# Loading and transforming the first batch of a spectral layer in finer pieces, with its weights behind the input and its tables placed by halves

## The chip, the cores and the metric

The kernel runs on one core of a Trainium2 chip. The metric is the device time of one execution in microseconds (us). TensorE is also called PE here (PEld is its weight load), VectorE is DVE, ScalarE is ACT, GpSimd is POOL and SyncE is SP, as the profile names them.

## The reference

```python
# x (8, 3008, 256); w_r, w_i (256, 256); b_r, b_i (256)
X = np.fft.rfft(x, axis=1);  Xr, Xi = X.real, X.imag
Yr = Xr @ w_r - Xi @ w_i + b_r
Yi = Xr @ w_i + Xi @ w_r + b_i
Y  = soft-threshold of Yr and Yi at 0.01
y  = np.fft.irfft(Y, n=3008, axis=1)
# then, over all 24064 rows of y, w_in (256, 2048), w_out (2048, 256)
r = np.maximum(y @ w_in, 0.0)
out = (s * r * r + b) @ w_out
```

## The kernel before

The length of 3008 is split as 94 x 32. The first DFT, over n1 (94 values), is a matmul with the table A_t. Its result ut is multiplied by W ("mix", into g), in pieces that are counted by u. A second DFT, over n2 (32 values), uses the tables F_t and F_2 and yields z after the soft threshold. The inverse DFT uses T_t. Then the MLP follows, which is most of the time. The first batch runs alone, in an order of its own; the batches behind it are woven into the MLP.

The tables are loaded in a compact form (F_c, T_c) and *placed* on the chip into zeroed tiles (F_t, F_2, T_t). W is loaded as f32 (w_st) and placed as f16 (W_t). The 256 features stand in two halves of 128, counted by dc. To evacuate a matmul's result is to copy it out of the accumulator (psh and the like), on ScalarE or VectorE.

```python
def emit_load_x(b):                       # GpSimd's queue, f32 -> f16
    for c in range(N2 // XCH):            # 4 chunks of XCH = 8 n2
        t = xpool.tile([P, XCH * D], F16, name="x16", tag="x16")
        nc.gpsimd.dma_start(out=t[0:N1, :], in_=xv[:, c * XCH * D : (c + 1) * XCH * D])
...
emit_load_x(0)
for w in (w_r, w_i):                      # SyncE's queue, beside x
    st = rpool.tile([P, DC, D], F32, name="w_st", tag="rt")
    nc.sync.dma_start(out=st, in_=w.rearrange("(c p) e -> p c e", p=P))
...
def first_batch():
    keep_awake(44)                        # matmuls on ones, for the clock
    for c in range(N2 // XCH):
        for dc in range(DC):
            ...                           # 8 matmuls into two banks
            for h in range(2):
                ... evac(ut[:, dc, :, n2 : n2 + 4], ...)   # ScalarE or VectorE
        keep_awake(18 if c < 3 else 12)
        if c == 1: ... emit_load_forward()                 # F_c, after this chunk's VectorE copies
        if c == 2: ... emit_load_inverse()                 # T_c
        if c == 2: ... place_w()                           # ScalarE
    place_f()                             # ScalarE, F_t from F_c
    place_f_2(0)                          # VectorE
    ...
    for i in range(2 * U + 2):            # U = 6; g of every third u is copied by ScalarE
        mix(*steps[i]); fwd_dft(*steps[i - 1]); inv_dft(*steps[i - 2]); ...
        if i == 0: ... place_t(0)         # VectorE
        if i == 2: ... place_f_2(1); place_t(1)
```

Of the kernel before, what the change touches and what calls it, by code (L numbers as in the profile page):

```python
# [14 lines left out]
P = 128  # L15
N1 = 94
N2 = 32
# [79 lines left out]
def kernel(  # L97
# [13 lines left out]
    nc = tc.nc  # L111
    B, S, D = x.shape
# [5 lines left out]
    H = NPAIR // 2  # L118
# [36 lines left out]
    def evac(dst, src, cols, scale=None):  # L155
        ta, td = 0.17 + cols / 1200.0, 0.15 + cols / 960.0
        if load["act"] + ta <= load["dve"] + td:
            load["act"] += ta
            if scale is None:
                return None, nc.scalar.copy(out=dst, in_=src)  # L160
            return None, nc.scalar.mul(out=dst, in_=src, mul=scale)
        load["dve"] += td
        if scale is None:
            return nc.vector.tensor_copy(out=dst, in_=src), None
        return nc.vector.tensor_scalar_mul(out=dst, in0=src, scalar1=scale), None

    def two_banks():
        return hpool.tile([P, 2, 512], F32, name="psh", tag="psh")
# [8 lines left out]
    XCH = 8  # L177
    x16 = {}

    def emit_load_x(b):  # L180
        xv = x[b].rearrange("(n1 n2) d -> n1 (n2 d)", n2=N2)
        for c in range(N2 // XCH):
            t = xpool.tile([P, XCH * D], F16, name="x16", tag="x16")
            nc.gpsimd.dma_start(  # L184
                out=t[0:N1, :], in_=xv[:, c * XCH * D : (c + 1) * XCH * D]
            )
            x16[(b, c)] = t

    ones = cpool.tile([P, P], F16, name="ones")
# [2 lines left out]
    def keep_awake(n):  # L192

        ps = other_bank()
        for _ in range(n):
            nc.tensor.matmul(ps[:, 0:P], ones, ones, start=True, stop=True)
# [6 lines left out]
    w_st = []  # L203
    for w in (w_r, w_i):
        st = rpool.tile([P, DC, D], F32, name="w_st", tag="rt")
        nc.sync.dma_start(out=st, in_=w.rearrange("(c p) e -> p c e", p=P))
        w_st.append(st)

    b_g = cpool.tile([P, 2, D], F32, name="b_g")
    nc.vector.memset(b_g, 0.0)  # L210
# [52 lines left out]
    nc.vector.memset(T_t, 0.0)  # L263
    F_2 = [uspool.tile([P, H, P], F16, name="F_2", tag="us") for _ in range(2)]
    for f in F_2:
        nc.vector.memset(f, 0.0)

    def make_bounds():
        for t, c in ((low, -LAM), (high, LAM)):
# [11 lines left out]
    def blocks(t):  # L281
        return t.rearrange("p q (r a k) -> p q r a k", r=2, a=2)

    def place_w():
        for i in range(2):
            nc.scalar.copy(out=W_t[:, :, i], in_=w_st[i])

    def place_f():
        for a in range(2):
            r = slice(64 * a, 64 * a + 64)  # L290
            nc.scalar.copy(out=blocks(F_t)[r, :, :, a], in_=F_c[r])

    def place_f_2(h):

# [8 lines left out]
    def place_t(h):  # L303
        q = slice(h * H, h * H + H)
        for i in range(4):
            r = slice(32 * i, 32 * i + 32)
            c = 64 * (i % 2)
            nc.vector.tensor_copy(out=T_t[r, q, c : c + 64], in_=T_c[r, q])
# [20 lines left out]
    def first_batch():  # L329
        ut = ypool.tile([P, DC, 96, N2], F16, name="ut", tag="yt")  # L330
        last_dve = last_act = None
        keep_awake(44)
        for c in range(N2 // XCH):
            for dc in range(DC):
                ps = two_banks()
                for j in range(XCH):
                    lo = j * D + dc * P
                    last_pe = nc.tensor.matmul(
                        ps[:, j // 4, (j % 4) * 96 : (j % 4) * 96 + 96],
                        x16[(0, c)][0:N1, lo : lo + P], A_t[0:N1, :],  # L340
                        start=True, stop=True,
                    )
                for h in range(2):
                    n2 = c * XCH + 4 * h
                    on_dve, on_act = evac(
                        ut[:, dc, :, n2 : n2 + 4],
                        ps[:, h, 0:384].rearrange("p (n k) -> p k n", k=96), 384,
                    )
                    last_dve = on_dve or last_dve
                    last_act = on_act or last_act  # L350
            with tc.issue_after(last_pe.ins):
                keep_awake(18 if c < 3 else 12)
            if c == 1:
                with tc.issue_after(last_dve.ins):
                    nc.vector.memset(F_c[0:1, 0, 0, 0:1], 0.0)
                emit_load_forward()
            if c == 2:
                with tc.issue_after(last_dve.ins):
                    nc.vector.memset(T_c[0:1, 0, 0:1], 0.0)
                emit_load_inverse()  # L360
            if c == 2:
                with tc.issue_after(last_act.ins):
                    place_w()
        with tc.issue_after(last_dve.ins), tc.issue_after(last_act.ins):
            place_f()
            place_f_2(0)

        gate = nc.gpsimd.tensor_copy(out=w_in_t[0][0:1, 0:1], in_=T_c[0:1, 0, 0:1])
# [11 lines left out]
        def mix(ec, u):  # L380
            ps = two_banks().rearrange("p h (j r e) -> p (h j) r e", j=2, r=2)
            for j in range(4):
                q = 4 * u + j
                for dc in range(DC):
                    nc.tensor.matmul(  # L385
                        ps[:, j], ut[:, dc, 4 * q : 4 * q + 4, :],
                        W_t[:, dc, :, ec * P : (ec + 1) * P],
                        start=(dc == 0), stop=(dc == DC - 1),
                    )
            g = vpool.tile([P, 4, 2, P], F16, name="g0", tag="v")  # L390
            if u % 3 == 1:
                nc.scalar.copy(out=g, in_=ps)
                load["act"] += 1.02
            else:
                g_last[0] = nc.vector.tensor_tensor(  # L395
                    out=g, in0=ps,
                    in1=b_g[:, :, ec * P : (ec + 1) * P].unsqueeze(1).to_broadcast([P, 4, 2, P]),
                    op=ALU.add,
                )
                load["dve"] += 1.2  # L400
            gs[(ec, u)] = g
# [83 lines left out]
        for i in range(2 * U + 2):  # L485
            if i < 2 * U:
                mix(*steps[i])
            if 0 <= i - 1 < 2 * U:
                fwd_dft(*steps[i - 1])
            if 0 <= i - 2 < 2 * U:  # L490
                inv_dft(*steps[i - 2])
            k = i - U - 2
            if 0 <= k < 4:
                turn(0, k)
            if 0 <= k - 1 < 4:
                last_dft(0, 8 * (k - 1))
            if i >= 2 * U:
                some(3)
            if i == 0:
                with tc.issue_after(g_last[0].ins):  # L500
                    place_t(0)
            if i == 2:
                with tc.issue_after(g_last[0].ins):
                    place_f_2(1)
                    place_t(1)
            if i == 9:

                gate = nc.gpsimd.tensor_copy(out=low[0:1, 0, 0:1], in_=vt[0:1, 1, 0, 0:1])
                with tc.issue_after(gate.ins):
                    make_w_g()  # L510
                    make_bounds()
# [377 lines left out]
```

## Time and profile before

| | before |
|---|---|
| time | 854.56 us, median of 3 executions (854.24 to 855.53); 854.43 with three more, run beside the changed kernel |
| span in the profile, TensorE busy | 853.9 us, 98% |
| first MLP matmul (L730) | 52.31 us in this profile |
| from there to the end of the span | 801.6 us |

A line of the timeline reads: start, length, engine, source line, operation, what it writes and reads, shapes, count, and in brackets how long the engine was idle before it and what ended that. "Stretches" are slices of 2 us with the busy time of PE, PEld, DVE, ACT and POOL (and their instruction counts), then the granted clock, the DMA share and GB/s.

The profiled execution itself took 855.68 us.

### The profile page before, as it was taken

How to read it: one execution, taken by the hardware profiler on the slowest of the kernel's cores; microseconds unless marked ns; L12 is line 12 of the kernel's file. 1: busy time of each engine (PE TensorE's matmuls, PEld its weight loads, DVE VectorE, ACT ScalarE, POOL GpSimd, SP SyncE). 2: the span in 40 equal slices, each digit the busy share in tenths (PEclk: the TensorE clock that was granted, in tenths of full speed). 3: DMA queues.
4: the chain of work that ended last, by engine and by line, in shares of the span. 5: the costliest groups of instructions: out<-in, count | busy, mean ns of one | idle time of the engine just before them, and what ended most of it. 6: DMA issues, size and time to landing. Idle time of an engine off the chain costs nothing.

```text
span 853.9 us, 17140 instructions
## 1 busy us (share of the span) xinstructions
PE 838.1 (98%) x6690; PEld 603.6 (71%) x6690; DVE 698.1 (82%) x1025; ACT 643.0 (75%) x856; POOL 32.4 (4%) x54
## 2 busy tenths in 40 slices
PE   8889999999999999999999999999999999999997
PEld 7757777777777766777667776777667777766765
DVE  6888987888878887888878888888977888776674
ACT  5688887787778887787777887787877778666663
POOL 3210000000000000000000000000000000000000
PEclk9999999999999999999999999999999999999999
DMA  7863456423672357423662247613354223411111
GB/s 170 154 148 100 102 157 172 121 75 94 169 191 62 93 138 198 113 80 97 164 174 78 75 106 183 186 41 90 101 154 118 63 78 96 112 32 38 38 44 50
DMA packets 104866, 95.07 MB, mean 111 GB/s; under 512 B 9422, under 2 KB 97234, under 8 KB 103442
## 3 DMA queue, kind: packets, MB, share of 16 engines
q1 hardware_dynamic: 98786, 79.57, 32.2%
q0 software_dynamic: 6000, 14.42, 10.6%
q8 instruction: 52, 0.85, 0.4%
q14 instruction: 28, 0.23, 0.1%
HBM read 52.54 MB, written 46.66 MB: 116 GB/s over the span
## 4 chain that ended last, share of the span: by engine, by line
PE 90%; DVE 4%; ACT 3%; DMA 1%; issue 1%; POOL 0%; DVEq 0%; ACTq 0%; POOLq 0%
PE psa L799 37%; PE psh L730 37%; PE psf L596 4%; PE psf L531 3%; PE psf L567 2%; PE psf L582 2%; PE psf L626 2%; PE psf L679 2%; DVE gt L744 1%; DMA x<-in_x_dram 1%; ACT rt L737 1%; PE psh L385 1%; DVE g L395 1%; ACT yt L160 1%; PE psf L416 0%
## 5 line engine op out<-in xcount | busy, mean ns | idle before, releaser
L737 ACT ACTIVATE rt<-psh 128x1024 f32<-128x1024 f32 (+2 forms) x384 | 387.1, 1009 | 115.7 <-PE psh L730 114.5
L744 DVE TENSOR_TENSOR gt<-rt 128x1024 f16<-128x1024 f32 (+2 forms) x323 | 386.6, 1200 | 99.3 <-ACT rt L737 98.7
L799 PE MATMUL psa<-w_out_t,gt 128*128 128x256 f16 (+1 forms) x3024 | 453.9, 272 | 0.1
L799 PEld LDWEIGHTS <-gt 128*128 128x128 f16 (+1 forms) x3024 | 301.0, 101 | 186.9 <-issue 1.7
L730 PE MATMUL psh<-yt,w_in 128*128 128x512 f16 (+1 forms) x1344 | 396.9, 378 | 0.0
L730 PEld LDWEIGHTS <-w_in 128*128 128x128 f16 x1536 | 142.7, 98 | 26.6 <-issue 1.7
L809 DVE SCALAR_TENSOR_TENSOR ost<-psa,s_bc,bias_bc 128x512 f32<-128x512 f32 (+1 forms) x96 | 70.9, 738 | 9.6 <-PE psa L799 8.2
L741 ACT ACTIVATE gt<-rt 128x1024 f16<-128x1024 f32 (+2 forms) x61 | 64.1, 1051 | 1.0
L601 DVE TENSOR_TENSOR ring<-psf,s 128x512 f16<-128x512 f32 x84 | 57.5, 685 | 3.5 <-PE psf L596 3.4
L160 ACT CAST v<-psf 128x512 f16<-128x512 f32 x80 | 46.5, 582 | 18.1 <-PE psf L626 18.1
L160 ACT CAST xf<-psf 128x512 f16<-128x512 f32 x82 | 48.0, 585 | 11.1 <-PE psf L567 11.1
L160 ACT CAST u<-psf 96x512 f16<-96x512 f32 x78 | 45.1, 580 | 12.3 <-PE psf L531 12.1
L730 PE MATMUL psh<-tail,w_in 128*128 128x512 f16 (+1 forms) x192 | 52.1, 353 | 0.0
L596 PE MATMUL psf<-W_g,xf 128*128 128x256 f16 x336 | 50.4, 273 | 0.0
L160 ACT CAST yt<-psf 128x480 f16<-128x480 f32 (+2 forms) x76 | 38.5, 518 | 14.4 <-PE psf L679 14.3
L531 PE MATMUL psf<-x,A_t 94*96 94x512 f16 x104 | 39.6, 381 | 1.7 <-ACT yt L160 0.5
L607 DVE TENSOR_TENSOR ring<-ring,high 128x512 f16<-128x512 f16 x84 | 35.5, 423 | 2.2
L608 DVE TENSOR_TENSOR ring<-ring 128x512 f16<-128x512 f16 x84 | 35.5, 422 | 1.9
L606 DVE TENSOR_TENSOR ring<-ring,low 128x512 f16<-128x512 f16 x84 | 35.4, 422 | 1.5
L596 PEld LDWEIGHTS <-xf 128*128 128x128 f16 x336 | 32.9, 98 | 3.7
L184 POOL DMA_DIRECT2D x<-in_x_dram x32 | 16.8, 526 | 461.3 <-PE psf L531 445.1
L679 PE MATMUL psf<-C_t,vs 96*128 96x96 f16 x448 | 32.9, 205 | 0.0
(83 smaller groups left out, 492.2 us busy)
## 6 DMA issues: line engine op xcount, KB each, us to landing
out_dram<-ost SPq DMA_DIRECT2D x152, 128.0 KB
x<-in_x_dram POOLq DMA_DIRECT2D x32, 376.0 KB, 5.8
ud<-u SPq DMA_DIRECT2D x28, 384.0 KB
us<-ud SPq DMA_DIRECT2D x28, 384.0 KB
vd<-v SPq DMA_DIRECT2D x42, 256.0 KB
vs<-vd SPq DMA_DIRECT2D x14, 768.0 KB
ring<-ring SPq DMA_DIRECT2D x280, 32.0 KB
out_dram<-ost SPq DMA_DIRECT2D x16, 120.0 KB
```

Source lines behind the costliest of these rows:

```text
L160: return None, nc.scalar.copy(out=dst, in_=src)
L531: nc.tensor.matmul(ps[0:96, :], A_t[0:N1, :], x16[(b, c)][0:N1, j * D : (j + 2) * D], start=True, stop=True,)
L596: nc.tensor.matmul(ps[:, r, :], xt[:, 2 - r, dc], W_g[:, dc, r], start=(dc == 0), stop=(dc == DC - 1),)
L601: nc.vector.tensor_tensor(out=t, in0=ps, in1=hold[i // 2][:, i % 2].unsqueeze(1).to_broadcast([P, 2, D]), op=ALU.add,)
L607: nc.vector.tensor_tensor(out=m, in0=m, in1=high, op=ALU.min)
L679: nc.tensor.matmul(ps[:, j * 96 : (j + 1) * 96], vs[(b, h)][:, k, ec * P : (ec + 1) * P], C_t, start=True, stop=True,)
L730: nc.tensor.matmul(o, w_in_t[dc][:, mc * P : (mc + 1) * P], r, start=(dc == 0), stop=(dc == DC - 1),)
L737: nc.scalar.activation(out=rt[:, :, 0:w], in_=ps[:, :, 0:w], func=AF.Relu)
L741: nc.scalar.activation(out=gt[:, :, 0:w], in_=rt[:, :, 0:w], func=AF.Square)
L744: nc.vector.tensor_tensor(out=gt[:, :, 0:w], in0=rt[:, :, 0:w], in1=rt[:, :, 0:w], op=ALU.mult)
L799: nc.tensor.matmul(ps[0:size, h, :], gts[(ti, mc // 2)][:, mc % 2, sub * size : (sub + 1) * size], w_out_t[:, mc, :], start=(mc == 0), sto ...
L809: nc.vector.scalar_tensor_tensor(out=ost[0:size, 0:k], in0=ps[0:size, 0:k], scalar=s_bc[0:size], in1=bias_bc[0:size, 0:k], op0=ALU.mult, o ...
```

## The change

Its intent is to start TensorE on x earlier and to keep the first batch from waiting for tables. x of batch 0 is loaded in halves of a chunk; the first DFT goes in groups of 4 n2, of which dc 0 is evacuated by ScalarE and dc 1 by VectorE; W is loaded behind the second group instead of beside x, and in halves; F_t and T_t are placed by halves; and the F_2 memsets go to GpSimd. The lines that only rename or regroup are cut.

```diff
     def emit_load_x(b):
+            parts = 2 if b == 0 else 1
+            w = XCH * D // parts
+            for i in range(parts):
+                nc.gpsimd.dma_start(... halves ...)
 ...
-        nc.sync.dma_start(out=st, in_=w.rearrange("(c p) e -> p c e", p=P))
+    def emit_load_w():
+        for e in (slice(0, P), slice(P, D)):
+            for w, st in zip((w_r, w_i), w_st):
+                nc.sync.dma_start(
+                    out=st[:, :, e], in_=w.rearrange("(c p) e -> p c e", p=P)[:, :, e]
+                )
 ...
-        nc.vector.memset(f, 0.0)          # F_2
+        nc.gpsimd.memset(f, 0.0)
 ...
-        keep_awake(44)
-        for c in range(N2 // XCH):
+        keep_awake(30)
+        for g in range(N2 // 4):
+            c, h = divmod(g, 2)
 ...                                       # 4 matmuls and one copy per dc
-                keep_awake(18 if c < 3 else 12)
+                keep_awake(7)
+            if h == 0:
+                continue
+            if c == 0:
+                with tc.issue_after(last_dve.ins):
+                    for st in w_st:
+                        nc.vector.memset(st[0:1, :, 0:D:P], 0.0)
+                emit_load_w()
 ...
             if c == 2:
                 with tc.issue_after(last_act.ins):
-                    place_w()
+                    place_w(0)
         with tc.issue_after(last_dve.ins), tc.issue_after(last_act.ins):
-            place_f()
+            place_w(1)
+            place_f(0)
 ...
+            if i == 1: ... place_f(1)
             if i == 2:
                     place_f_2(1)
+            if i == 3:
                     place_t(1)
```

More of the change, by code (lines that the diff above doesn't have):

```diff
@@ L183, in emit_load_x @@
             t = xpool.tile([P, XCH * D], F16, name="x16", tag="x16")
-            nc.gpsimd.dma_start(
-                out=t[0:N1, :], in_=xv[:, c * XCH * D : (c + 1) * XCH * D]
-            )
+            parts = 2 if b == 0 else 1
+            w = XCH * D // parts
+            for i in range(parts):
+                nc.gpsimd.dma_start(
+                    out=t[0:N1, i * w : (i + 1) * w],
+                    in_=xv[:, c * XCH * D + i * w : c * XCH * D + (i + 1) * w],
+                )
             x16[(b, c)] = t
@@ L205 @@
         st = rpool.tile([P, DC, D], F32, name="w_st", tag="rt")
-        nc.sync.dma_start(out=st, in_=w.rearrange("(c p) e -> p c e", p=P))
         w_st.append(st)
+    def emit_load_w():
[3 more added lines that the diff above has]
+                    out=st[:, :, e], in_=w.rearrange("(c p) e -> p c e", p=P)[:, :, e]
+                )
     b_g = cpool.tile([P, 2, D], F32, name="b_g")
@@ L282, in blocks, with place_w, place_f @@
         return t.rearrange("p q (r a k) -> p q r a k", r=2, a=2)
-    def place_w():
+    def place_w(ec):
+        e = slice(ec * P, ec * P + P)
         for i in range(2):
-            nc.scalar.copy(out=W_t[:, :, i], in_=w_st[i])
-    def place_f():
+            nc.scalar.copy(out=W_t[:, :, i, e], in_=w_st[i][:, :, e])
+    def place_f(h):
+        q = slice(h * H, h * H + H)
         for a in range(2):
             r = slice(64 * a, 64 * a + 64)
-            nc.scalar.copy(out=blocks(F_t)[r, :, :, a], in_=F_c[r])
+            nc.scalar.copy(out=blocks(F_t)[r, q, :, a], in_=F_c[r, q])
     def place_f_2(h):
@@ L331, in first_batch @@
         last_dve = last_act = None
-        keep_awake(44)
-        for c in range(N2 // XCH):
+        keep_awake(30)
+        for g in range(N2 // 4):
+            c, h = divmod(g, 2)
             for dc in range(DC):
-                ps = two_banks()
-                for j in range(XCH):
-                    lo = j * D + dc * P
+                ps = two_banks()[:, 0]
+                for j in range(4):
+                    lo = (4 * h + j) * D + dc * P
                     last_pe = nc.tensor.matmul(
-                        ps[:, j // 4, (j % 4) * 96 : (j % 4) * 96 + 96],
+                        ps[:, j * 96 : j * 96 + 96],
                         x16[(0, c)][0:N1, lo : lo + P], A_t[0:N1, :],
@@ L342, in first_batch @@
                     )
-                for h in range(2):
-                    n2 = c * XCH + 4 * h
-                    on_dve, on_act = evac(
-                        ut[:, dc, :, n2 : n2 + 4],
-                        ps[:, h, 0:384].rearrange("p (n k) -> p k n", k=96), 384,
-                    )
-                    last_dve = on_dve or last_dve
-                    last_act = on_act or last_act
-            with tc.issue_after(last_pe.ins):
-                keep_awake(18 if c < 3 else 12)
+                on_dve, on_act = evac(
+                    ut[:, dc, :, 4 * g : 4 * g + 4],
+                    ps[:, 0:384].rearrange("p (n k) -> p k n", k=96), 384,
+                )
+                last_dve = on_dve or last_dve
+                last_act = on_act or last_act
+            with tc.issue_after(last_pe.ins):
+                keep_awake(7)
[6 more added lines that the diff above has]
+                emit_load_w()
             if c == 1:
@@ L391, in mix @@
             if u % 3 == 1:
-                nc.scalar.copy(out=g, in_=ps)
+                g_last[0] = nc.scalar.copy(out=g, in_=ps)
                 load["act"] += 1.02
@@ L501, in first_batch @@
                     place_t(0)
+            if i == 1:
+                with tc.issue_after(g_last[0].ins):
+                    place_f(1)
             if i == 2:
@@ L504, in first_batch @@
                     place_f_2(1)
+            if i == 3:
+                with tc.issue_after(g_last[0].ins):
                     place_t(1)
```

## The prediction

> **What bounds the kernel now.** I read the page first, then the chain of waits that ended last over the first 60 us, then the timeline of the first 40 us, then the clock by stretches of 2 us. The page's first lines say where time can be won:
>
> ```profile
> span 853.9 us, 17140 instructions
> ...
> PE 838.1 (98%) x6690; PEld 603.6 (71%) x6690; DVE 698.1 (82%) x1025; ACT 643.0 (75%) x856; POOL 32.4 (4%) x54
> ...
> PE 90%; DVE 4%; ACT 3%; DMA 1%; issue 1%; POOL 0%; DVEq 0%; ACTq 0%; POOLq 0%
> ```
>
> TensorE is busy 98% of the span and is 90% of the last chain. The change touches only the first batch, up to about 54 us, where the long run of L730 and L799 begins. After that the order of instructions of the two kernels agrees on every engine (line numbers aside). So the change can only shift when the long TensorE phase starts, by less than the some 20 us in which the first batch waits for something. 2% would be 17.1 us; that is out of reach.
>
> In the first 26 us the last chain reads (start, length, what):
>
> ```profile
> 1.87 7.16 DMA x<-in_x_dram
> ...
> 11.15 0.04 DVE F_c L355
> 11.21 3.68 DMA F_c<-dft_fwd
> ...
> 14.96 1.47 ACT F_t L291
> 16.45 1.47 ACT F_t L291
> ...
> 24.38 1.24 DVE g L395
> ```
>
> So it is: the load of x; the VectorE copies of ut (10.13 to 11.15) that let a memset release the load of F_c; that load; the placing of F_t on ScalarE in two pieces of 1.47 us; the mix copy g behind it (17.94), for which the forward DFT waits until 17.97; then VectorE, where four T_t pieces (22.90 to 24.35) stand ahead of the next g. The timeline adds how the four chunks of x arrive and what TensorE does:
>
> ```profile
> 6.59 0.85 PE L338 MATMUL psh<-A_t,x 94*128 94x96 f16 x16 [0.67 <-DMA x<-in_x_dram]
> ...
> 13.08 0.85 PE L338 MATMUL psh<-A_t,x 94*128 94x96 f16 x16
> ...
> 14.14 1.02 DVE L164 CAST ut<-psh 128x384 f16<-128x384 f32 x2 [0.97 <-ACT ut L160]
> ...
> 24.55 0.49 PE L385 MATMUL psh<-W_t,ut 128*128 128x256 f16 x3 [1.10 <-ACT g L392]
> ```
>
> Chunks start on TensorE at 6.59, 9.07, 11.09 and 13.08, two us apart, although nothing on TensorE holds them: x comes at the pace of the DMA engines. The last ut copy ends at 14.14 + 1.02 = 15.16, 2.1 us after its chunk began, because VectorE waits for ScalarE (the releaser in brackets). The clock by stretches (PEclk is the value after the POOL counts) has one hole:
>
> ```profile
> 26.00:28.00 2.00, 2.00 (x19) 1.42 (x17) 1.18 (x3) 1.16 (x2) 0.00 (x0) 0.65 1.05 207
> 28.00:30.00 2.00, 2.00 (x17) 1.69 (x16) 1.38 (x2) 1.16 (x2) 0.00 (x0) 0.50 1.09 219
> ```
>
> The granted clock halves from about 26.7 to 30.1 us, after the idle TensorE of 24 to 26 us (0.83 of 2 us busy).
>
> **What the Trainium skill says.** "TensorE: Matmul & The Clock Gate", part 1, "The HAM clock gate": the clock is half until a busy window of 3413 ns has passed, and falls back after an idle one; the window runs free of the kernel. The trace agrees: the 44 first matmuls on ones take 4.61 us, 105 ns each, the later ones 57 ns each (18 in 1.03 us), and the hole is 3.4 us long. The keep-awake matmuls serve this, and the change cuts them. "DMA: Bandwidth & Descriptors", "Queues, rings and completion order": each DMA engine goes round robin between the rings it has work for. The records agree in part: from 6 to 8 us W and x packets alternate (14 of 1024 B to 12 of 4096 B in a quarter us), but from 4.0 to 5.0 us x went almost alone. "VectorE: DVE Perf Modes", "Zero memsets can be issued as uint32": a memset takes one cycle per element, so as uint32 it has half the elements. VectorE's memset of one F_2 half is 128x768 uint32 at 0.75 us. On GpSimd it is 128x1536 f16; I estimate 1.3 to 1.8 us each, no run so far shows it.
>
> **The change part by part.**
>
> 1. x in halves. A chunk is 94 packets of 4096 B at 0.322 us over 16 engines, 1.9 us; a half is 94 packets that I estimate at 0.165 us, 0.97 us. The first group can start after one half, and W (512 KB, 512 packets of 1024 B at 46 ns, 1.5 us of all engines) no longer goes ahead. With a first packet at 2.9 us and 0.65 us from the last packet to TensorE (as at 12.4 to 13.08 now), groups land at 4.5, 5.5, 6.5 us and so on. TensorE starts 2.1 us earlier than 6.59.
>
> 2. W moves behind the second group: issued at about 7.5, first packet 1.1 us later as F_c shows (11.21 to 12.3), at 8.6. It is now 1024 packets of 512 B. The us loads at 65 to 70 us are such packets: 27 ns each. That is 1024 x 27 / 16 = 1.7 us, 0.2 more than before. Interleaved with the rest of x it delays the end of x by about 0.5 us: 2.9 + 7.8 + 0.5 = 11.2, last group on TensorE at 11.9 against 13.08. The first halves of W land at about 12.4, all of W at 13.3.
>
> 3. The copies side by side. dc 0 goes to ScalarE, dc 1 to VectorE, each waiting for TensorE alone; after the last matmul 1.2 us instead of 2.1. Taken alone this gives ut at 13.1. But ScalarE is strict in order, and its W placing (two copies, about 0.4 us each) stands ahead of the last two groups' copies. It can't start before 12.4. So ScalarE copies group 6 at 13.2, group 7 at 13.9, and mix starts at about 14.7 against 14.76 and 15.21 now. **Most of the 2 us of the x load is lost here**: 0.3 us is left.
>
> 4. F_c queues behind W in the same ring. All bytes before it are those of before, plus 0.2 us for smaller packets; it lands at about 15.1, not 14.88. Cost 0.2 us.
>
> 5. Tables by halves. F_t(0) is two pieces of 0.74 us, 1.47 us less ahead of g on ScalarE, less 0.3 for W's second half: F_t(0) ends at 16.7 instead of 17.92. The first mix copy on VectorE ends at 15.2 + 0.9 + 1.24 = 17.3, so the forward DFT begins at 17.4 instead of 17.97. Gain 0.55 us.
>
> 6. T_t(1) moves behind u = 3. VectorE now runs T_t(0) to 18.8, g to 20.0, two z to 21.3, F_2(1) to 22.15, g(3) to 23.4. Before, g(3) ended at 25.62. Gain 2.2 us on that g; the T_t(1) pieces come after z(2), 24.1 to 25.5, and hold z(3) to 25.6 against 27.02: of the 2.2 about 1.4 to 1.6 us stays.
>
> 7. Clock. TensorE is no longer idle around 24 to 26 us, so the hole should not follow. In it the chain was on TensorE from 25.66; up to 1.7 us (half of 3.4) could be won, much of it hidden behind ScalarE and VectorE; I count 0.5 us.
>
> 8. GpSimd memsets: 5 to 10 us, ahead of F_2 at 15.2: hidden. Two VectorE memsets of 0.75 us leave before the first group, where they would delay the copy of 5 us.
>
> Sum: the gains of 1 to 5 are the 0.55 us at the forward DFT; with part 6, 1.5 us; with the clock 2.0. I take off 0.4 us for my own optimism (no waits between parts): **1.6 us, 854.56 - 1.6 = 853.0 us**.
>
> **Rivals.**
> A. The W placing is the new wait. If W lands at 13 or later, ScalarE keeps groups 6 and 7, TensorE idles from 11.6 to 13.7, and a clock window falls in it: then the mix matmuls run at half clock, 16 x 0.11 us becomes 3.5 us, and 1.5 us goes. For it: the fewer keep-awake matmuls (86 against 110), and that W is strictly behind x. Against it: a window with 72% busy (9.66 less 6.25, 2.46 us of 3.41) kept the clock. It makes 854.5 to 855.
> B. W lands by 12, because it takes its turns between the x packets fully, as in 6 to 8 us now. Then nothing of part 3 is lost, ut is there at 13.2, and F_c becomes the only bound: 851 to 852.
> C. The first 50 us are hidden anyway, by the load of x(1) and the MLP weights that starts when T_c lands. Against it: those are issued by 22 us and land by about 39, and their first reader stands at 45 us. The chain from 34 to 54 us runs over TensorE, ScalarE and VectorE in turn, with no DMA in it. I give it little.
>
> **Range and chances.** Run to run 854.24 to 855.53, the clock window being free-running. My parts are uncertain by 0.5 us at the landing of W and of F_c and by 1 us at the clock. 851.2 to 854.9 should hold 8 in 10. Either 2% bound would need 17 us: 0.5% each.
>
> **What would show it.** x: first L338-type matmul at 4.5 us instead of 6.59, groups about 1 us apart. W: the ScalarE copy W_t waits for DMA at 10.5 to 12.5, and the copies of ut behind it start late. F_c landing at 15.0 to 15.3. Forward DFT at 17.4, the fourth g ended at 23.4, first L730 at about 50.5 instead of 52.31. Clock: no half-clock stretch between 20 and 35 us. It is wrong if a half-clock stretch falls on the mix (rival A), if ut is complete before 13.5 (rival B), or if first L730 moves and the end does not (rival C).

## The result, and the profile after

The changed kernel took 854.8 us (median of 6 fast executions, 854.4 to 857.06), the kernel before 854.43 (854.16 to 855.53) in the same rounds. The ratio is 1.0006, 95% interval 0.9993 to 1.0019: the same. Ratios here are the mean time of one kernel's fast runs over the mean of the other's fast runs of the same rounds, so not quite the ratio of the medians. The forecast was a gain of 1.6 us; none came.

The page of the changed kernel, with the lines that answer to those of before:

```profile
span 853.2 us, 17109 instructions
...
PE 836.9 (98%) x6666; PEld 601.8 (71%) x6666; DVE 696.9 (82%) x1025; ACT 644.0 (75%) x860; POOL 37.3 (4%) x60
...
PE 91%; DVE 4%; ACT 3%; DMA 1%; issue 1%; DVEq 0%; ACTq 0%; POOLq 0%
```

Nothing on the page tells the kernels apart. The chain of waits over the first 30 us does (start, length, what):

```profile
7.63 5.77 DMA w_st<-in_w_r_dram
...
13.49 0.16 ACT W_t L299
...
14.63 0.78 PE psh L353 x8
...
16.16 2.77 PE psh L406 x16
...
18.95 1.01 ACT g L413
```

Before, this stretch of the chain ran over x, the ut copies and F_c. Now it runs over **the load of W**, issued at 7.63 and landed 5.77 us later, then over ScalarE's placing of W, a copy of ut, the last x group (at 14.63) and the mix. The timeline shows how one waits for the other:

```profile
4.85 0.51 PE L353 MATMUL psh<-A_t,x 94*128 94x96 f16 x8 [0.43 <-DMA x<-in_x_dram]
...
13.49 0.71 ACT L299 CAST W_t<-w_st 128x256 f16<-128x256 f32 x2 [1.97 <-DMA w_st<-in_w_r_dram]
...
14.11 0.47 ACT L160 CAST ut<-psh 128x384 f16<-128x384 f32 x1
14.63 0.78 PE L353 MATMUL psh<-A_t,x 94*128 94x96 f16 x8 [2.00 <-ACT ut L160]
...
15.95 2.96 PE L406 MATMUL psh<-W_t,ut 128*128 128x256 f16 x16
...
19.18 0.22 PE L437 MATMUL psf<-g,F_t 128*128 128x128 f16 x1 [0.26 <-DVE g L416]
```

ScalarE stands 1.97 us before W_t although its next copy of ut, behind it in its order, could run. TensorE then stands 2.00 us for that copy. The first group did start early (4.85, before 6.59), but the last one started at 14.63, later than before (13.08). The 16 mix matmuls took 2.96 us. In the stretches, the clock tells why (first the kernel before, then the changed one):

```profile
14.00:16.00 2.00, 1.67 (x20) 1.23 (x18) 1.78 (x6) 1.52 (x3) 0.00 (x0) 1.00 0.77 216
16.00:18.00 2.00, 1.06 (x11) 0.71 (x9) 1.79 (x3) 1.97 (x3) 0.60 (x2) 1.00 0.49 134
```

```profile
14.00:16.00 2.00, 1.37 (x16) 1.36 (x15) 0.55 (x1) 1.45 (x5) 0.00 (x0) 0.67 0.82 288
16.00:18.00 2.00, 2.00 (x12) 1.41 (x10) 0.96 (x6) 1.87 (x3) 0.40 (x2) 0.50 0.36 110
```

The granted clock is 0.67 and 0.50 where before had 1.00 from 14 to 18 us. In this execution no hole follows at 26 to 30 us; half clock lies on the mix instead. The load of F_c, which queues behind W, came late too. VectorE, which reads F_c beside ScalarE, waited for it until 16.29 us, where in the kernel before F_c had landed at 14.89 (11.21 + 3.68):

```profile
16.29 0.25 DVE L312 TENSOR_SCALAR F<-F_c 64x384 f16<-64x384 f16 x1 [0.29 <-DMA F_c<-dft_fwd]
```

The profile of before was of one of the longer executions, so I ran that kernel once more, unchanged, to have one of a common execution (854.30 us, a single run, so its state is unknown):

> The kernel before, unchanged, for a second trace. Of its ten timed executions two took 855.3 to 855.7 us, and eight 854.1 to 854.5; the first profile came from one of the two slow ones and has a half-clock stretch from 26.7 to 30.1 us. If the stretch is what made it slow, this profile, if it falls among the common ones, shows no half clock between 6 and 850 us, the same times up to 25 us (forward DFT at 17.9 to 18.1) and the first matmul of the MLP at 50.8 to 51.2 us instead of 52.3, with the span at 852.4. If the common executions differ earlier than 25 us, the stretch was not the cause.

Its stretch after 26 us, and its first MLP matmul beside that of the first profile and that of the changed kernel:

```profile
26.00:28.00 2.00, 1.98 (x27) 1.54 (x25) 1.18 (x3) 1.26 (x3) 0.00 (x0) 1.00 1.08 215
...
51.03 0.38 PE L730 MATMUL psh<-yt,w_in 128*128 128x512 f16 x1
```

```profile
52.31 0.38 PE L730 MATMUL psh<-yt,w_in 128*128 128x512 f16 x1
```

```profile
51.71 0.38 PE L756 MATMUL psh<-yt,w_in 128*128 128x512 f16 x1
```

In the common execution of before the clock is 1.00 there, although TensorE had been even less busy just before, from 24 to 26 us (0.72 of 2 us, against 0.83 in the first profile). In the changed kernel it is idle there as well (0.92 of 2 us busy). First the common execution of before, then the changed kernel:

```profile
24.00:26.00 2.00, 0.72 (x8) 0.52 (x8) 1.96 (x4) 0.60 (x1) 0.00 (x0) 1.00 1.03 205
```

```profile
24.00:26.00 2.00, 0.92 (x13) 0.70 (x11) 1.96 (x5) 1.74 (x3) 0.00 (x0) 1.00 1.08 215
```

The MLP of the common execution starts 1.3 us earlier than in the profile that the prediction was read from. Against the common one, the changed kernel starts its MLP 0.68 us *later* (51.71 against 51.03). From the first MLP matmul to the end of the span it is 801.5 us in both.

### The profile page after: what moved, and what is told of

It is laid out like the page before. It is cut to its first block, busy times and chain, and to the rows that moved or that the text cites. A ratio compares the mean times of both kernels' runs of the same rounds, so it can differ in the third digit from the quotient of the medians.

```text
span 853.2 us, 17109 instructions
## 1 busy us (share of the span) xinstructions
PE 836.9 (98%) x6666; PEld 601.8 (71%) x6666; DVE 696.9 (82%) x1025; ACT 644.0 (75%) x860; POOL 37.3 (4%) x60
## 4 chain that ended last, share of the span: by engine, by line
PE 91%; DVE 4%; ACT 3%; DMA 1%; issue 1%; DVEq 0%; ACTq 0%; POOLq 0%
PE psa L825 37%; PE psh L756 37%; PE psf L622 4%; PE psf L557 3%; PE psf L593 2%; PE psf L608 2%; PE psf L652 2%; PE psf L705 2%; DVE gt L770 1%; ACT rt L763 1%; PE psh L406 1%; DMA w_st<-in_w_r_dram 1%; ACT yt L160 1%; ACT vs L160 0%; DMA x<-in_x_dram 0%
## 5 line engine op out<-in xcount | busy, mean ns | idle before, releaser
L160 ACT CAST u<-psf 96x512 f16<-96x512 f32 x78 | 45.1, 580 | 12.3 <-PE psf L557 12.1
L187 POOL DMA_DIRECT2D x<-in_x_dram x36 | 18.9, 528 | 461.2 <-PE psf L557 445.1
```

Of the source, the lines that this page charges most:

```text
L160: return None, nc.scalar.copy(out=dst, in_=src)
```

## The experiments

All kernels gave correct results. Kernels named together ran on the same chip and share the runs of the kernel before (854.2 to 854.3 us in each series). There are four series: e1 to e4; e5 to e8; e9, t1 and x1 with the repeat above; t2 and t3. The first three ran on one chip, the fourth on another. Of the ten runs of before that e5 to e8 are compared with, nine are those of e1 to e4. "Slower" and "faster" below mean an interval that leaves out 1.

### First series: the wait for W, and the clock

**e1, W placed after all x groups** (changed kernel with one edit). It takes away ScalarE's wait in the middle of the x groups.

```diff
-            if c == 2:
-                with tc.issue_after(last_act.ins):
-                    place_w(0)
         with tc.issue_after(last_dve.ins), tc.issue_after(last_act.ins):
+            place_w(0)
             place_w(1)
```

> The changed kernel with one edit: the first half of W is placed by ScalarE after the last copies of ut instead of ahead of those of groups 6 and 7. Theory A (the in-order wait of ScalarE for W is where the gain went): ut is complete at 12.9 us, TensorE does not stand from 12.6 to 14.6 us, the mix starts at about 14.3 us (W lands at 13.5, two copies of 0.37 us) instead of 15.95, no half-clock stretch covers the mix, the forward DFT begins at 17.2 instead of 19.2, the first matmul of the MLP 1 to 1.5 us earlier, the time 0.8 to 1.5 us below the changed kernel's 854.8, that is 853.3 to 854.0. Rival D (the first 25 us are hidden behind VectorE's own queue of F_2, T_t and g): the mix is earlier but the fourth g still ends at 25.7 us and the time stays within 0.4 us of 854.8.

Measured: 854.21 us, ratio to before 0.9999 (0.9986 to 1.0011). That is 0.6 us below the changed kernel's median, but the intervals overlap. The profile shows something else that was in none of the theories:

```profile
9.97 0.84 PE L353 MATMUL psh<-A_t,x 94*128 94x96 f16 x8
10.62 0.95 PE L200 MATMUL psa<-ones 128*128 128x128 f16 x7
11.36 0.84 PE L353 MATMUL psh<-A_t,x 94*128 94x96 f16 x8
...
13.02 0.56 PE L200 MATMUL psa<-ones 128*128 128x128 f16 x7
...
15.90 1.91 PE L404 MATMUL psh<-W_t,ut 128*128 128x256 f16 x16 [0.37 <-ACT W_t L299]
```

Seven matmuls on ones take 0.95 us up to about 12 us and 0.56 us after it, so in this execution TensorE worked at half clock until 12 us (the clock's records begin at 12.10), and groups came 1.39 us apart (9.97, 11.36). TensorE itself was now the pace of the x groups. The wait for W was hidden behind that, and the mix ran at 15.90 at full clock. This gave a new theory, E: the 30 keep-awake matmuls, cut from 44, are too few to release the clock in time.

**e2, forty more matmuls on ones behind group 6**, to keep the clock up while ScalarE waits for W.

```diff
-                keep_awake(7)
+                keep_awake(47 if g == 6 else 7)
```

> The changed kernel with 47 instead of 7 keep-awake matmuls after group 6 (40 more, 2.3 us at full clock), which fill TensorE's wait for ScalarE from 12.6 to 14.6 us and nothing else. Theory B (the half clock is where the gain went): no half-clock stretch between 14 and 19 us, the 16 mix matmuls take 1.8 us instead of 2.96, the forward DFT begins at about 18.0 instead of 19.2, and the time falls by 0.7 to 1.2 us to some 853.8. Theory A: the mix still starts at about 15.7 us, the time falls by less than 0.5 us. Rival D: no change at all.

Measured: 855.66 us, ratio 1.0018 (1.0004 to 1.0032): slower, by less than 2%. It is a miss as an experiment. In the profile half clock lasted to 12 us again, W had landed by the time ScalarE came to it, and the added matmuls themselves held the last group to 16.56 us. In this execution the keep-awake matmuls stood in front of the work and cost it most of their own length (2.79 us).

**e3, all of W at the start** as in the kernel before, the rest as in the changed kernel.

```diff
+        nc.sync.dma_start(out=st, in_=w.rearrange("(c p) e -> p c e", p=P))
 ...
-            if c == 0:
-                with tc.issue_after(last_dve.ins):
-                    for st in w_st:
-                        nc.vector.memset(st[0:1, :, 0:D:P], 0.0)
-                emit_load_w()
```

> The changed kernel with W loaded whole ahead of x, as in the kernel before, all else kept (halves of x, groups of four, copies side by side, tables by halves). Theory A and C (the late load of W is the cause): ScalarE never waits for W, the groups of x start about 1 us later than in the changed kernel (5.8 instead of 4.85) and the last one at about 12.6, ut complete at 13.5, mix at 13.6 to 13.9, the load of F_c lands at 15.0, the forward DFT begins at 17.2, the time falls to 853.0 to 853.8. Rival D: the stages are earlier and the time stays within 0.4 us of 854.8.

Measured: 854.7 us, ratio 1.0004 (0.9991 to 1.0016). Taken alone this would clear the load of W. But its executions spread over 853.64 to 855.51, and in the profiled one (855.28) half clock ran from 7 to 14 us. With 30 keep-awake matmuls the kernel has no margin, and this experiment couldn't tell the two causes apart.

**e4, half of W at the start, half behind the second group**, and the second half placed at step 4 of the loop, before the mix that reads it.

```diff
+    emit_load_w(slice(0, P))
 ...
-                emit_load_w()
+                emit_load_w(slice(P, D))
 ...
-            place_w(1)
+            if i == 4: ... place_w(1)
```

> The changed kernel with the first halves of W (columns 0 to 127) loaded ahead of x, the second halves where the change has them, and their placing moved from ahead of F_t to the fifth mix. Theory A: ScalarE has W before it needs it and nothing of W stands ahead of F_t; ut complete at 13.2, mix at 13.3, F_c lands at 14.9, F_t(0) placed by 16.5, forward DFT at 16.9, time 852.7 to 853.5, the best of the four. Rival D: within 0.4 us of 854.8. If it is no better than the run with W whole ahead of x, F_c alone sets the forward DFT.

Measured: 853.85 us, ratio 0.9991 (0.9978 to 1.0003). ut was complete at 13.99 and the mix began at 13.62, so the x groups no longer waited for anything but their own pace. The next wait was F_c, the subject of the prediction's part 4:

```profile
15.45 1.67 ACT L305 COPY F_t<-F_c 64x768 f16<-64x768 f16 x2 [1.96 <-DMA F_c<-dft_fwd]
```

### Second series: 64 keep-awake matmuls, to take the early clock out of it

Each of these is an earlier kernel with one number changed, except e8.

```diff
-        keep_awake(30)
+        keep_awake(64)
```

**e5: the changed kernel with 64.**

> The changed kernel with 64 instead of 30 keep-awake matmuls at the start. Theory E (the 30 cover too little of a 3.4 us clock window, so in some executions TensorE stays at half clock up to 12 us and each group of x takes 1.39 us of it instead of 0.98): the half clock is over by 8 us at the latest in every execution, the last group of x starts by 13.5 us in the profile even where the clock was late; but ScalarE still waits for W (copies W_t at 13.3), so the mix starts at 15.5 to 16.0 and the median falls little: 854.2 to 854.7, with the spread of the five runs under 0.8 us instead of 2.7. Theory A says the same of the median. If the late load of W were nothing, this alone would bring 853.5 or less.

Measured: 855.92 us, ratio 1.002 (1.0007 to 1.0034): slower than before, and theory E in its simple form falls. The early half clock is gone from the profile (groups start 0.9 to 1.0 us apart), and the wait for W is worse:

```profile
14.59 0.71 ACT L299 CAST W_t<-w_st 128x256 f16<-128x256 f32 x2 [2.41 <-DMA w_st<-in_w_r_dram]
...
15.73 0.80 PE L353 MATMUL psh<-A_t,x 94*128 94x96 f16 x8 [2.39 <-ACT ut L160]
```

The load of W is issued after the second group's copies. Those come later when 64 matmuls stand ahead (8.70 us, not 7.63), so W lands a microsecond later, TensorE idles 2.39 us, and the mix runs at half clock (2.76 us). All five executions had a mean clock of 0.996 or 0.997.

**e6: e1 with 64** (W still behind x, but placed after the groups).

> The changed kernel with 64 keep-awake matmuls at the start and the first half of W placed after the last copies of ut. In the first run with late placing TensorE was at half clock up to 12.2 us, so that run did not show what the wait for W costs. Theory A with E: ut complete at 12.9 to 13.3, mix at 14.2 to 14.4 (W lands at 13.5), forward DFT at 17.0 to 17.3, median 853.2 to 853.8. Rival (the load of W itself is too late, placing order does not matter): mix at 15.5 or later, 854.3.

Measured: 854.27 us (4 executions), ratio 1.0002 (0.9988 to 1.0015). Against e5, from the same series and with only the place of place_w different, this is 1.65 us less. **ScalarE's order, W's placing ahead of the last two groups' copies, costs 1.65 us, the clock that falls with it included.** One of e6's four executions had a mean clock of 0.997 (all five of e5 had 0.996 or 0.997); it took 855.44 us, 0.48 below e5's median. So by this one execution most of the 1.65 us is half clock that the wait brings on.

**e7: e4 with 64.**

> First halves of W loaded ahead of x, second halves placed late (as in the earlier run of that name), and 64 keep-awake matmuls. Theory A with E: mix at 13.5 to 14.0, then F_c is the bound (lands at 15.3 to 15.5, behind the second half of W), forward DFT at 17.5 to 17.7, median 853.0 to 853.4 (profile of the run before: 852.96), spread under 0.8 us.

Measured: 852.95 us (4 executions), ratio 0.9985 (0.9971 to 0.9999). With W out of the way the longer keep-awake seems to pay: 0.9 us below e4, though across two series and with overlapping intervals. Within e7, three executions had a mean clock of 1.0 and took 852.66 to 853.06 us, one had 0.997 and took 853.95.

**e8: e7 with the second half of W behind both tables**, so that F_c need not queue behind it.

```diff
-            if c == 0: ...                # this block moves
-                emit_load_w(slice(P, D))
             if c == 2:
                 ...
                 emit_load_inverse()
+                ...
+                emit_load_w(slice(P, D))
```

> As the run with the first half of W ahead of x and 64 keep-awake matmuls, but the second half of W is loaded behind F_c and T_c. If F_c waits in the queue behind the second half of W (256 KB, 512 packets at 27 ns over 16 engines, 0.86 us), it now lands at 14.3 to 14.6, the forward DFT begins at 16.6 to 16.9 and the median falls to 852.2 to 852.7. If F_c only waits for the end of x, it lands at 15.3 again and the time is that of the other run.

Measured: **852.54 us** (6 executions, 852.21 to 852.78), ratio 0.9978 (0.9966 to 0.9991). This is the best of all, 2.3 us below the changed kernel and 1.8 us below before (854.29 in its series). F_c's placing moved forward from 15.33 (e7) to 14.17 us and waits for no load. Against e7 the medians differ by 0.41 us, with overlapping intervals; in the profiles the MLP starts 0.67 us earlier (49.12 against 49.79):

```profile
14.17 1.67 ACT L305 COPY F_t<-F_c 64x768 f16<-64x768 f16 x2
...
49.12 0.38 PE L757 MATMUL psh<-yt,w_in 128*128 128x512 f16 x1
```

### Third and fourth series: each part on its own

**e9: e3 with 64** (all of W at the start), the counterpart to e5.

> The changed kernel with 64 keep-awake matmuls and W whole ahead of x: against the run with 64 and W where the change has it (855.92) it differs in the place of the load of W alone. Theory A with C (the late load of W is what ate the gain): no wait of ScalarE for W, mix at 14.0 to 15.0 instead of 17.07, forward DFT at 17.3 to 17.8 instead of 20.28, and since 801.4 us follow the first matmul of the MLP in all runs and 32.3 us lie between the forward DFT and it, a span of about 851.0 to 851.6, that is 852.8 to 853.4 us. Rival: the halves of x and groups of four are at fault; then it stays above 854.5.

Measured: 853.61 us, ratio 0.9994 (0.9981 to 1.0008). e5 and e9 differ only in the load of W, behind the second group in halves or at the start whole: 855.92 and 853.61, or 1.0020 and 0.9994 of their own runs of before. **The load of W behind x costs 2.3 us** with this keep-awake, again with its half clock: the one execution of e9 at 0.997 took 855.37 us, 0.55 below e5's median. In e9's profile (which fell on its one execution of 855.37 us, half clock on the mix) W_t waits for nothing, and a late x group waits for x:

```profile
12.06 0.71 ACT L300 CAST W_t<-w_st 128x256 f16<-128x256 f32 x2
...
13.78 0.51 PE L354 MATMUL psh<-A_t,x 94*128 94x96 f16 x8 [1.53 <-DMA x<-in_x_dram]
```

**t1: the kernel before with only the tables by halves.**

```diff
-            place_f()
+            place_f(0)
 ...
-                nc.scalar.copy(out=g, in_=ps)
+                g_last[0] = nc.scalar.copy(out=g, in_=ps)
 ...
+            if i == 1: ... place_f(1)
+            if i == 3: ... place_t(1)      # was at i == 2
```

> The kernel before with the tables by halves alone: F_t placed in two halves, the second after the second mix, T_t's second half after the fourth mix. x, its groups, W and the keep-awake matmuls as before. My part 5: F_t(0) done at 16.6 instead of 17.9, forward DFT at 17.45 instead of 17.97. My part 6: the fourth g ends at 23.7 to 24 instead of 25.6. With 32.3 us from the forward DFT to the MLP, as in all runs with this order, the MLP begins at 49.8 to 50.0 and the median is 852.9 to 853.2. Rival (the order of the tables gives nothing against an execution of before without a half-clock stretch): 853.8 to 854.3.

Measured: 853.05 us (852.82 to 853.4), ratio 0.9984 (0.9971 to 0.9997), beside 854.21 for before: 1.16 us gained. F_t(0), first in the common execution of before and then in t1:

```profile
15.07 2.95 ACT L291 COPY F_t<-F_c 64x1536 f16<-64x1536 f16 x2 [0.95 <-DMA F_c<-dft_fwd]
```

```profile
15.16 1.67 ACT L292 COPY F_t<-F_c 64x768 f16<-64x768 f16 x2 [1.12 <-DMA F_c<-dft_fwd]
...
49.62 0.38 PE L736 MATMUL psh<-yt,w_in 128*128 128x512 f16 x1
```

The forward DFT starts at 17.36 instead of 18.08, and the MLP at 49.62 instead of 51.03: half of the 1.4 us comes before the forward DFT and half after it.

**x1: the kernel before with only x in halves and groups of 4** (keep-awake 44 at the start and 9 or 6 behind a group; W at the start, tables whole, memsets on VectorE).

```diff
+            parts = 2 if b == 0 else 1     # x in halves
 ...
-        for c in range(N2 // XCH):
+        for g in range(N2 // 4):
+            c, h = divmod(g, 2)
 ...
-                keep_awake(18 if c < 3 else 12)
+                keep_awake(9 if c < 3 else 6)
```

> The kernel before with the halves of x, the groups of four n2 and the copies side by side alone: W whole ahead of x, 44 keep-awake matmuls at the start and 9 (then 6) a group, F_2 memsets on VectorE, tables whole. If x comes at the pace of the DMA engines, its end stays at 12.4 to 13.2 us; the last copy of ut ends 1.2 instead of 2.1 us after its group began, at 14.2 to 14.6; F_c is issued at 10.5 instead of 11.2 and lands at 14.3 to 14.8; then F_t whole holds the forward DFT to 17.4 to 17.8: 0.2 to 0.5 us gained, 853.8 to 854.1. If copies side by side were worth the 1 us of my part 3, 853.3.

Measured: 855.5 us, ratio 1.0014 (1.0 to 1.0028): 1.3 us longer than before, where no loss had been in sight. ut was complete at 14.81 (before 14.80), and the forward DFT at 18.06 (before 18.08). So up to there the change of x is worth nothing. The loss comes later, as a stretch of half clock:

```profile
26.00:28.00 2.00, 2.00 (x13) 1.46 (x13) 1.18 (x2) 1.23 (x2) 0.00 (x0) 0.50 1.07 215
```

Four of its five executions had a mean clock of 0.997 and took 855.21 to 855.59 us, no more than the longer executions of before with that mean clock (855.34 to 855.65). But the fifth had 1.000 and took 856.12, so the hole goes with the loss and is not shown to be all of it. On VectorE the two kernels differ in the loop only in the order of one z and one g; why the hole is met so often stays open.

**t2: t1 with half of W at the start and half behind the tables**, that is e8 without anything done to x.

```diff
-        nc.sync.dma_start(out=st, in_=w.rearrange("(c p) e -> p c e", p=P))
+    emit_load_w(slice(0, P))
 ...                                        # c == 2, after emit_load_inverse()
+                emit_load_w(slice(P, D))
 ...
+            if i == 4: ... place_w(1)
```

> The kernel before with the tables by halves and the first half of W ahead of x, the second behind F_c and T_c and placed after the fifth mix; x in whole chunks, copies and keep-awake matmuls as before. Against the best so far (852.54, the same with halves of x, groups of four, copies side by side and memsets on GpSimd). If the groups are worth something once W is out of the way: 853.0, that is 0.4 us slower than that. If not: 852.3 to 852.6, with the last chunk of x starting at 12.0 to 12.3, ut complete at 14.1 to 14.4, F_c landed at 14.3 to 14.8, forward DFT at 16.7 to 17.1.

Measured: 852.62 us (852.05 to 852.95), ratio 0.9981 (0.9967 to 0.9994), the same as e8 (0.9978), which ran in another series and on another chip.

**t3: x1 and t1 together.**

> The tables by halves, with the halves of x, the groups of four and the copies side by side: the tables-only kernel (853.05) with the groups put on, W whole ahead of x, 44 and 9 or 6 keep-awake matmuls, memsets on VectorE. The groups alone gave 855.5, with a half-clock stretch at 25.9 us in the profile that the tables-only kernel does not have. If that stretch is what the groups lost, it is gone here (TensorE has work at 23 to 25 us with the tables by halves): forward DFT at 17.3 to 17.5, 852.9 to 853.3, equal to tables only. If the groups cost something of their own, the last group of x starts 0.5 to 1 us later than with whole chunks (13.71 against 12.63 there), the mix follows, and it is 853.5 to 854.2.

Measured: 853.83 us, ratio 0.9994 (0.9981 to 1.0006). The half clock of x1 is gone from the profile. It is 1.2 us slower than t2 of the same series, which has the halves of W and lacks the change of x. t1, in another series and on another chip, was at 0.9984. So groups of 4 and halves of x show no gain here, and by the medians seem to cost about 0.8 us (853.83 against 853.05); as the intervals overlap, that cost is not shown. In the profile the last group waits for its data:

```profile
14.41 0.51 PE L344 MATMUL psh<-A_t,x 94*128 94x96 f16 x8 [1.05 <-DMA x<-in_x_dram]
```

In the trace's records of packets, the last three packets of x ended at 12.59, 13.50 and 13.71 us, among those of F_c, while the rest were done by 12.51. In t1 and t2 the last x packet ended at 12.20 and 11.89.

### The stages side by side

Starts from the profiles in us; the last two columns are the time of the profiled execution and the median. Rows marked * had half clock on the mix or after it, rows marked + before 14 us.

| kernel | last x group | mix | forward DFT | MLP | profiled | median |
|---|---|---|---|---|---|---|
| before, first profile * | 13.08 | 14.76 | 17.97 | 52.31 | 855.68 | 854.43 |
| before again | 12.71 | 14.39 | 18.08 | 51.03 | 854.30 | |
| changed * | 14.63 | 15.95 | 19.18 | 51.71 | 854.98 | 854.80 |
| e1 + | 14.39 | 15.90 | 18.65 | 50.90 | 854.08 | 854.21 |
| e2 + | 16.56 | 17.47 | 19.98 | 52.38 | 855.59 | 855.66 |
| e3 + | 15.91 | 16.81 | 19.39 | 51.74 | 855.28 | 854.70 |
| e4 | 12.64 | 13.62 | 17.65 | 49.90 | 852.96 | 853.85 |
| e5 * | 15.73 | 17.07 | 20.28 | 52.63 | 855.87 | 855.92 |
| e6 * | 14.38 | 15.90 | 19.26 | 52.23 | 855.44 | 854.27 |
| e7 | 13.79 | 14.71 | 17.53 | 49.79 | 853.06 | 852.95 |
| e8 | 13.35 | 14.26 | 16.77 | 49.12 | 852.31 | 852.54 |
| e9 * | 14.70 | 15.89 | 19.12 | 51.87 | 855.37 | 853.61 |
| t1 | 12.63 | 14.31 | 17.36 | 49.62 | 852.89 | 853.05 |
| x1 * | 13.71 | 14.61 | 18.06 | 51.92 | 855.21 | 855.50 |
| t2 | 12.31 | 13.99 | 16.80 | 49.07 | 852.38 | 852.62 |
| t3 | 14.41 | 15.32 | 17.83 | 50.18 | 854.10 | 853.83 |

From the first MLP matmul to the end of the span, 801.3 to 801.7 us pass in all of them, and 802.15 in t3. So what the first batch gains or loses at the MLP's start shows in the time.

## Why the prediction was right or wrong

The gain of 1.6 us did not come. The step that failed is 2, the landing of W behind x. Through it the costs in 3 and 4 came out too small, and 7 counted a gain that was not there to be had. Times of packets are given here from the start of the span, as in the timeline; the prediction's own readings of packets and of the clock lie about 0.1 us later. The steps, by their numbers:

**1, x in halves: right in size, wrong in worth.** The first group started at 4.85 us (4.5 said), packets of 2048 B took 173 ns (165 said). But the last x packet ended at 12.28, not 11.2, and the kernel before had its last at 12.60 in the first profile and 12.33 in the common one. x1 shows what an earlier first group is worth: nothing at the forward DFT (18.06 against 18.08).

**2, W behind the second group: this step failed.** W was issued at 7.63, as said, but its first packet came at 9.87, not 8.6. The step let W take its turns with x packets. In the records 50 of W's 1024 packets were through by 11.4 us, while 125 x packets had started since 9.87. Eight tenths of W started between 11.57 and 13.25, once x was nearly through, and its last packet ended at 14.58. ScalarE's first half of W landed at 13.40, not 12.4. The prediction had the sign in its own records: from 4.0 to 5.0 us of the kernel before, 3 packets of W went beside 50 of x. It noted this and built on the stretch of 6 to 8 us, where they alternate.

**3, the copies side by side: right about ScalarE's order, too small in what it costs.** W's placing stood in front of the copies of groups 6 and 7 as described; ScalarE stood still for 1.97 us and TensorE for 2.00 us. With the landing a microsecond later, the mix began at 15.95, not 14.7, and at half clock. With 64 keep-awake matmuls e5 and e6 put 1.65 us on this order, e5 and e9 2.3 us on the load's place with it, and e6 and e9 still had an execution each near 855.4 with half clock. With the change's own 30, moving the placing gave 0.6 us (e1) and loading W whole at the start 0.1 us (e3) by the medians, neither clear of noise. Only with half of W at the start (e4, 0.95 us less) was every execution shorter than every one of the changed kernel, and that was in another series. The 0.65 us between 1.65 and 2.3 is not tied to one thing.

**4, F_c: wrong as well.** The step had the whole of W ahead of F_c at a cost of 0.2 us, with F_c landing at 15.1. In the changed kernel VectorE waited for it until 16.29, about 1.2 us more. ScalarE, which was placing W until 16.21, hid most of this. In e4, with half of W ahead of F_c, the placing of F_c began at 15.45; in e8, with none, at 14.17.

**5 and 6, tables by halves: right.** The prediction had 1.5 us for parts 1 to 6 together; t1, which has only 5 and 6, starts the MLP 1.41 us earlier and is 1.16 us faster. Its forward DFT starts at 17.36 (17.4 said), although a piece of F_t(0) takes 0.83 us and not 0.74. The fourth g ends 2.1 us earlier (23.63 against 25.71), with 2.2 said. From the forward DFT to the MLP t1 takes 32.26 us, the common execution of before 32.95, and the changed kernel 32.53, so there 0.42 of the 0.69 us is kept. It is paid away before the forward DFT, which starts at 19.18 instead of 18.08.

**7, the clock: wrong by its baseline and in its reason.** The hole at 26.6 to 30.0 us belonged to the profiled execution (855.68 us), not to the kernel: the common execution has none, and 29 of 33 executions took 854.0 to 854.6. There was nothing to gain in the median. The reason given was that TensorE would no longer be idle at 24 to 26 us. It was busy for 0.92 of 2 us there, against 0.83 in the first profile, and for 0.72 in the common execution, which kept its clock. So that the changed kernel shows no hole there is no success of the step. The prediction itself gave the range of 854.24 to 855.53 and called the window free-running; it should have asked which of the two the profile was.

**8, memsets on GpSimd: right.** They are hidden, and two take 2.71 us, 1.36 each (1.3 to 1.8 said):

```profile
6.46 2.71 POOL L278 MEMSET F<- 128x1536 f16 x2
```

**The rivals.** Rival A is what happened, in its chain and in its time: W landed after 13 us, TensorE idled 2.00 us, a window of half clock fell on the mix, and 854.8 lies in its 854.5 to 855. The prediction gave it too little. One of its arguments against A was a window 72% busy that had kept the clock; by the clock's records that window is 6.13 to 9.54 us, 68% busy. It did not bear: the window that lost the clock here (11.27 to 14.68 us) was 41% busy. Rival B, W by 12 us, is refuted; e4 and e8 get near it by loading half of W at the start. Rival C is refuted by the constant 801.3 to 801.7 us.

**In one sum:** tables −1.16 us by t1; the change as a whole +0.37 us by medians, which is within noise; so the other parts cost about 1.5 us (two series set against each other), where the prediction had them at nothing to a gain of 0.5 (the clock).

**What stays open.** The records show that W hardly got turns beside x, not why: a fetch ahead in the queue and the order of service would look alike. How much of the changed kernel's time the half clock on the mix costs is not isolated. In e6, e7 and e9 the one execution with a mean clock of 0.997 took 1.1 to 1.8 us longer than the others, but in the changed kernel the one with 1.000 took 854.49 against a median of 854.8. That mean is no safe sign with 30 keep-awake matmuls: e1's profiled execution has 1.000 as well, though it ran at half clock until 12.1 us. No run here set the phase of the clock. Whether e8 needs 64 keep-awake matmuls or would do with 44 was not tried, and t2 reaches the same time with 44.

## What to carry to other kernels

Move a load behind another only if nothing in a strictly ordered engine stands between its reader and work on the path: here a copy that waited for W held two copies that did not need it, and 1.65 us went in that order and the half clock that came with it. When a load is moved to make room for an earlier start, check first that the *last* piece of the data ahead of it comes earlier; here the first piece was worth nothing by itself (x1). And before counting on a hole in a profile, ask whether the profiled execution took the median time.

## What the Trainium skill lacked or had wrong

- "TensorE: Matmul & The Clock Gate", part 1, "The HAM clock gate", says that the clock is released after a busy window of 3413 ns and lost after an idle one, and gives no share of busy time. Counted in windows of 3.41 us from the recorded changes of each trace, up to 30 us, TensorE's busy share does not decide it. In e4 a window 80% busy (1.74 to 5.15 us) released the clock; in e1 windows 80% and 83% busy (1.86 to 5.27 and 5.27 to 8.69, the second 2.83 of 3.41 us) did not. Windows 41%, 50% and 57% busy lost it (changed kernel, first profile of before, e6), while windows 47%, 52% and 57% busy kept it (e4, e6, the common execution of before).
- The same section puts the penalty, as a start-up cost, below 1% of a span. The runs agree in size (1.1 to 1.2 us, or 0.1%, within e6 and e7), but that is as large as the gain of t1.
- The same part warns, in its caveats on HAM traces, that clock events in a trace can be unreliable, but not that a profile may miss the half clock at the start. In e1 the clock column reads 1.00 for 10 to 12 us, while seven matmuls on ones took 0.95 us there against 0.56 us later. The durations of one form tell it.
- "DMA: Bandwidth & Descriptors", "Queues, rings and completion order", has each DMA engine go round robin between its rings by packet. Beside x, issued by GpSimd, the load of W issued by SyncE had 50 of the trace's packets through from 9.87 to 11.4 us while 125 went for x. That is not one for one, and the section doesn't say what a load that joins late must expect.
- The same page, "Specifications", puts the latency to the first byte at about 0.6 us for the path of SyncE and ScalarE. Measured from issue to first packet, W behind x took 2.2 us, F_c in the kernel before 1.0 us.
- No page that I found gives the time of a GpSimd memset: 128x1536 f16 took 1.36 us each here.
